# Attention heads in pairs, nine tokens of one head per partition, one burst in row halves, and MLP sums in borrowed PSUM banks

## The chip, the cores and the metric

The kernel runs on one core of a Trainium2 chip. The metric is the device time of one execution, in microseconds (us), as the median over the executions of a kernel.

Engines have short names. PE is the matmul engine (TensorE) and PEld is its weight load. DVE is VectorE, ACT is ScalarE, POOL is GpSimd and SP is SyncE. PSUM is the memory that PE sums into, and it is divided into banks.

## The reference, cut to what matters

```python
def phi(x):                                   # x: q or k times a scale
    proj = np.einsum('bhsd,md->bhsm', x, omega)      # 64 -> 128 features
    h = proj - np.sum(x * x, axis=-1, keepdims=True) / 2.0
    h = h - np.max(h, axis=-1, keepdims=True)
    return np.exp(h) / np.sqrt(m)
q_p, k_p = phi(q_s), phi(k_s)                 # 8 batches, 8 heads, 576 tokens
kv  = np.einsum('bhsm,bhsd->bhmd', k_p, v)    # called k'v below
z   = np.sum(k_p, axis=2)
out = einsum(q_p, kv) / (einsum(q_p, z) + 1e-06)
x   = out as 4608 tokens x 512
g   = h * sigmoid(1.702 * h), with h = x @ w_in  # 512 -> 2048, "first layer"
y   = g @ w_out                                  # 2048 -> 512, "second layer"
```

## The kernel before

The MLP works in nine blocks of 512 tokens. One chunk of its first layer is four 128x512 matmuls into a PSUM bank (`ph`), a tanh on ACT (`th`), and a gate on DVE (`gT`), which reads `th` and `ph`. The attention of later tokens is woven between these matmuls. From block 2 on, PE does the first layer of block i, the second layer of block i-1, and the attention of four pairs of heads (one batch) in the same stretch. I call the part of that stretch that belongs to one pair of heads a round.

Attention runs head by head. k lies with six tokens per partition on 96 partitions. The projections use the two row halves of PE (64 rows each), and k'v uses all rows. The division of k' by its maximum is moved onto v (`vp`).

```python
ps_pp = ctx.enter_context(tc.tile_pool(name="ps_pp", bufs=2, space=PSUM))
ps_m = ctx.enter_context(tc.tile_pool(name="ps_m", bufs=1, space=PSUM))
banks = [ctx.enter_context(tc.tile_pool(name=f"ps_b{j}", bufs=1, space=PSUM)) for j in range(3)]
# (cut) item_qk, one head:
        pk = ps_pp.tile([128, 2, 512], F32, name="pk", tag="pp")
        pq = ps_pp.tile([128, 2, 512], F32, name="pq", tag="pp")
        for c in range(3):
            for lo in (0, 64):
                nc.tensor.matmul(pk[:, lo // 64, c * 128 : (c + 1) * 128], lhsT=kT[lo : lo + 64, ...], rhs=omT2[lo : lo + 64, :])
        for lo in (0, 64):
            nc.tensor.matmul(pq[:, lo // 64, 0:S2], lhsT=omT2[lo : lo + 64, :], rhs=qT[lo : lo + 64, :])
        for _ in range(warmers):     # 6 fillers a head in the head of the program
            nc.tensor.matmul(pq[:, 0, S2:512], lhsT=warm[:, 0:128], rhs=warm[:, S2:512])
        # (cut) exp of k and q on ACT; maximum, reciprocal and v' on DVE or POOL
# (cut) item_kv:
            for t in range(6):
                nc.tensor.matmul(kv[:, i, :], lhsT=ke[:, t, :], rhs=vp[:, t, :], start=(t == 0), stop=(t == 5))
# (cut) the MLP's first layer: one-bank tiles, shared with nobody from block 1 on
            phs[i, f] = banks[j].tile([128, TB], F32, name="ph", tag=f"b{j}")[:]
```

The softmax here doesn't subtract the row's maximum and nothing guards it: scores larger than these inputs give would overflow.

## Time and profile before

| | before |
|---|---|
| median of 2 runs | 338.39 us (337.62 to 339.16) |
| span of the profiled run | 335.6 us |
| PE busy | 96% |
| first tanh of block 0 / block 2 / block 7 | 28.45 / 91.67 / 264.12 us |

The starts of the tanh instructions on ACT are used here to cut the span into stages: a head, an early part up to block 2, and a steady part.

First, lines of the profile's page: the span, busy time by engine, PE and clock by 40 equal slices (in tenths; 9 means 90% or more), and the chain of waits.

```profile
span 335.6 us, 6767 instructions
...
PE 322.2 (96%) x2562; PEld 170.1 (51%) x2606; DVE 229.8 (68%) x551; ACT 203.0 (60%) x363; POOL 83.4 (25%) x162
...
PE   7999899999999999999999999999999999999996
...
PEclk9999999999999999999999999999999999999999
...
PE 78%; DMA 10%; ACT 4%; DVE 4%; issue 2%; POOL 1%; SPq 0%; POOLq 0%; ACTq 0%; DVEq 0%
```

PE is busy at full clock nearly everywhere, and the chain that ended last is 78% PE. A change has to take work off PE.

The list of what PE waited for (waiting instruction, what released it, us in total, times, longest us) shows no wait that repeats in every round. Its two largest entries:

```profile
PE warm_ps L90 <- DVE warm L86: 1.5, 1, 1.5
PE kv L240 <- POOL vp L226: 1.2, 3, 0.5
```

The timeline shows the attention of one pair among the MLP's matmuls (start, duration, engine, line, tiles, count).

```profile
138.42 0.35 PE L185 MATMUL pk<-omT,qk 64*128 64x128 bf16 x6
...
141.69 0.35 PE L185 MATMUL pk<-omT,qk 64*128 64x128 bf16 x6
...
142.97 0.55 PE L240 MATMUL kv<-vp,ke 96*128 96x65 bf16 x12
```

Each head has its own burst of projections (the six for k are shown). One stretch of twelve k'v matmuls follows for the pair.

### The profile page before, as it was taken

The numbers are of one execution on the slowest core, as the hardware profiler recorded it, in microseconds if no ns is written. First come the engines' busy times: TensorE is split into PE (matmuls) and PEld (weight loads), VectorE is DVE, ScalarE is ACT, GpSimd is POOL, SyncE is SP. The second block draws the span as 40 slices with busy tenths as digits, with TensorE's granted clock in tenths as the row PEclk, the third lists the DMA queues.
The fourth block names the chain that finished last, engine by engine and source line by source line (L and its number), as shares of the span: only waits on it lengthen the run. The fifth ranks groups of instructions, "written<-read, shape, count | busy, mean of one in ns | idle before, by whom it ended". The sixth has DMA issues, their size and how long they took to land.

```text
span 335.6 us, 6767 instructions
## 1 busy us (share of the span) xinstructions
PE 322.2 (96%) x2562; PEld 170.1 (51%) x2606; DVE 229.8 (68%) x551; ACT 203.0 (60%) x363; POOL 83.4 (25%) x162
## 2 busy tenths in 40 slices
PE   7999899999999999999999999999999999999996
PEld 3764455554445444555445555554545444444444
DVE  2887886989888877887788868886887334444300
ACT  4977867778766656665666666665665444344411
POOL 8882455302250115111511041000101011001010
PEclk9999999999999999999999999999999999999999
DMA  8999998997699619993898269941212110101022
GB/s 180 238 227 255 249 187 124 163 236 139 91 219 186 139 47 219 192 128 76 198 195 155 66 155 182 193 92 51 51 51 50 51 31 31 64 31 31 33 73 84
DMA packets 59412, 43.31 MB, mean 129 GB/s; under 512 B 44020, under 2 KB 54260, under 8 KB 58740
## 3 DMA queue, kind: packets, MB, share of 16 engines
q0 software_dynamic: 10320, 21.86, 32.3%
q1 hardware_dynamic: 48852, 20.72, 30.8%
q8 instruction: 20, 0.33, 0.4%
q10 hardware_dynamic: 208, 0.29, 0.3%
q14 instruction: 12, 0.10, 0.1%
HBM read 36.73 MB, written 15.34 MB: 155 GB/s over the span
## 4 chain that ended last, share of the span: by engine, by line
PE 78%; DMA 10%; ACT 4%; DVE 4%; issue 2%; POOL 1%; SPq 0%; POOLq 0%; ACTq 0%; DVEq 0%
PE po L351 33%; PE ph L325 30%; DMA qk<-in_q_dram 5%; PE pk L185 4%; PE kv L240 3%; PE nd L255 2%; DMA xt<-xb 2%; PE pq L191 2%; DMA out_dram<-osb 2%; ACT ke L195 1%; DMA qk_f<-in_k_dram 1%; ACT qe L197 1%; PE po L372 1%; PE pq L193 1%; POOL vp L220 1%
## 5 line engine op out<-in xcount | busy, mean ns | idle before, releaser
L325 PE MATMUL ph<-xt,win 128*128 128x512 bf16 x555 | 145.9, 380 | 2.5 <-DVE gT L339 0.5
L351 PE MATMUL po<-wout,gT 128*128 128x512 bf16 x537 | 139.0, 379 | 2.0 <-issue 0.5
L338 ACT ACTIVATE th<-ph 128x512 bf16<-128x512 f32 x144 | 85.7, 598 | 87.7 <-PE ph L325 86.0
L339 DVE SCALAR_TENSOR_TENSOR gT<-th,ph 128x512 bf16<-128x512 bf16 x144 | 97.1, 679 | 58.1 <-ACT th L338 55.7
L325 PEld LDWEIGHTS <-win 128*128 128x128 bf16 x576 | 59.3, 114 | 50.6 <-issue 5.5
L351 PEld LDWEIGHTS <-gT 128*128 128x128 bf16 x560 | 50.1, 98 | 55.9 <-issue 5.8
L363 POOL DMA_DIRECT2D out_dram<-osb x44 | 23.3, 533 | 174.8 <-ACT osb L360 140.6
L195 ACT ACTIVATE ke<-pk 96x768 bf16<-96x768 f32 x64 | 51.4, 803 | 13.9 <-PE pk L185 13.9
L197 ACT ACTIVATE qe<-pq 128x576 bf16<-128x576 f32 x64 | 41.3, 646 | 1.1 <-PE pq L193 1.1
L258 DVE TENSOR_TENSOR xb<-nd,rden 128x320 bf16<-128x320 f32 x64 | 31.1, 486 | 1.3
L360 ACT ACTIVATE osb<-po 128x512 f32<-128x512 f32 x35 | 20.9, 598 | 16.0 <-PE po L351 15.7
L220 POOL TENSOR_TENSOR vp<-vst,emax 96x384 bf16<-96x384 f32 x20 | 16.6, 830 | 36.7 <-PE ph L325 20.5
L214 DVE TENSOR_REDUCE maxE<-half 96x6 f32<-96x384 bf16 x44 | 24.2, 549 | 1.4
L220 DVE TENSOR_TENSOR vp<-vst,emax 96x384 bf16<-96x384 f32 x44 | 24.3, 552 | 1.0
L255 PEld LDWEIGHTS <-qe 128*128 128x128 bf16 x320 | 17.7, 98 | 13.7 <-DVE xb L258 1.7
L213 DVE TENSOR_TENSOR half<-ke 96x384 bf16<-96x384 bf16 x44 | 15.6, 354 | 10.9 <-ACT ke L195 10.8
L240 PEld LDWEIGHTS <-ke 96*128 96x128 bf16 x384 | 16.7, 98 | 8.5 <-issue 2.9
L240 PE MATMUL kv<-vp,ke 96*128 96x65 bf16 x384 | 19.1, 194 | 1.8 <-POOL vp L226 1.2
L255 PE MATMUL nd<-kvs,qe 128*128 128x65 bf16 x320 | 20.3, 194 | 0.6 <-DVE xb L258 0.6
L210 DVE TENSOR_REDUCE maxE<-ke 96x6 f32<-96x768 bf16 x20 | 18.8, 940 | 2.7 <-ACT ke L195 2.7
L185 PEld LDWEIGHTS <-qk 64*128 64x128 bf16 x240 | 7.3, 102 | 16.9 <-issue 16.9
L257 DVE RECIPROCAL rden<-nd 128x5 f32<-128x5 f32 x64 | 11.8, 185 | 3.4 <-PE nd L255 3.1
(48 smaller groups left out, 192.5 us busy)
## 6 DMA issues: line engine op xcount, KB each, us to landing
vst<-in_v_dram SPq DMA_DIRECT2D x5, 1152.0 KB, 7.7
out_dram<-osb POOLq DMA_DIRECT2D x12, 256.0 KB, 2.3
sk<-in_k_dram POOLq DMA_DIRECT2D x20, 144.0 KB, 7.3
sq<-in_q_dram POOLq DMA_DIRECT2D x20, 144.0 KB, 7.7
vst<-in_v_dram SPq DMA_DIRECT2D x4, 576.0 KB, 13.2
win<-in_moe_w_in_dram POOLq DMA_DIRECT2D x2, 1024.0 KB, 14.5
wout<-in_moe_w_out_dram POOLq DMA_DIRECT2D x4, 512.0 KB, 17.8
out_dram<-osb POOLq DMA_DIRECT2D x10, 192.0 KB, 2.7
```

The costliest lines, as they stand in the source:

```text
L195: nc.scalar.activation(out=ke[:], in_=pk[0:KP, :, 0:384], func=AF.Exp, scale=SCALE)
L197: nc.scalar.activation(out=qe[:].rearrange("p (two r) -> p two r", two=2), in_=pq[:, :, 0:S2], func=AF.Exp, scale=SCALE,)
L214: nc.vector.reduce_max(out=maxE[:], in_=half[:], axis=AX.X)
L220: eng.tensor_tensor(out=vp[:, :, 0:64].rearrange("p (two c) d -> p two c d", two=2), in0=tiles[b]["v"][:, h, :].rearrange("p (c two d) -> ...
L240: nc.tensor.matmul(kv[:, i, :], lhsT=ke[:, t, :], rhs=vp[:, t, :], start=(t == 0), stop=(t == 5))
L255: nc.tensor.matmul(nd[:, t, :], lhsT=qe[:, c0 : c0 + 128], rhs=kvs[:, i, :])
L258: nc.vector.tensor_tensor(out=xb[:, :, i * 64 : (i + 1) * 64], in0=nd[:, :, 0:64], in1=rden[:].unsqueeze(2).to_broadcast([128, NCH, 64]), ...
L325: nc.tensor.matmul(ph, lhsT=win[f // 8][:, c, f % 8 // 4 * 512 + f % 4 : (f % 8 // 4 + 1) * 512 : 4], rhs=xt[c][:, i * TB : (i + 1) * TB], ...
L338: nc.scalar.activation(out=th[:], in_=ph, func=AF.Tanh, scale=0.851)
L339: nc.vector.scalar_tensor_tensor(out=gT[:, f, :], in0=th[:], scalar=1.0, in1=ph, op0=ALU.add, op1=ALU.mult)
L351: nc.tensor.matmul(po[:], lhsT=gT[:, f, r * 128 : (r + 1) * 128], rhs=wout[:, f, :], start=(f == 0), stop=(f == NFC - 1),)
L363: eng.dma_start(out[row : row + (n - 1) * step + 1 : step, :], osb[p0 : p0 + n, :])
```

## The change

The intent is less PE time for attention and less work on DVE. Two heads share the 128 partitions, 64 each, with nine tokens per partition. All row-half work of a pair is then one burst: nine k projections, the q projections, and the k'v of the pair before as two streams of nine matmuls in the two halves. Matmuls of different halves may run side by side, and the change into and out of half mode is paid once a pair.

The burst needs wide PSUM tiles, so the banks are cut anew. There are three two-bank tiles (`kp`, `qp`, `xx`) and two single banks. Between bursts, MLP sums borrow the two banks of `kp` as the two halves of one tile (`f:kp`, `f:kp+`). The fillers in the head are dropped.

```diff
+    psum = {
+        n: ctx.enter_context(tc.tile_pool(name=f"ps_{n}", bufs=1, space=PSUM))
+        for n in ("kp", "qp", "xx", "b0", "b1")
+    }
-    WARMERS = 6
...
+    def item_tr(p, home=None, on_act=(False, True)):
+            both = bank("qp", [128, 2, 1024], BF16, "tps")
+            tpk, tpq = both[:, 0, :], both[:, 1, :]
...
+        copy(on_act[0], kT[:], tpk[:, 0:640])
...            six transposes of q into tpq
+        copy(on_act[1], qT[:], tpq[:, 0 : 2 * S2])
...
+    def item_burst(p, kvp=None):
+        for s in range(2):
+            row = [(56, lambda s=s, j=j: proj_k(s, j)) for j in range(4)]
+            row.append((216, lambda s=s: proj_q(s, False)))
+            row.append((29, lambda s=s: proj_q(s, True)))
+            if s == five:
+                row.append((56, lambda s=s: proj_k(s, 4)))
+            if kvp is not None:
+                row += [(30, mm) for mm in kv_mms(xx, kvp, s)]
...            the two rows are issued merged by their times
+        nc.scalar.activation(out=ke[:, 0:8, :]..., in_=pk[:]..., func=AF.Exp, scale=SCALE)
+        nc.scalar.activation(out=qes[:, :, :, 0:256], in_=pq[:]..., func=AF.Exp, scale=SCALE)
+        nc.scalar.activation(out=ke[:, 8, :], in_=xx[:, five, 256:384], func=AF.Exp, scale=SCALE)
...
     def mm1(i, f, c0=0, c1=CM):
+            if homes[i, f][-1] == "+" and (i, f - 1) in readers:
+                for reader in readers[i, f - 1]:
+                    tc.declare_no_dep(mm.ins, reader.ins.name, reason="another PSUM bank")
...
+        readers[i, f] = [
+            nc.scalar.activation(out=th[:], in_=ph, func=AF.Tanh, scale=0.851),
+            nc.vector.scalar_tensor_tensor(
+                out=gT[:, f, :], in0=th[:], scalar=1.0, in1=ph, op0=ALU.add, op1=ALU.mult
+            ),
+        ]
...
+    R5 = "B f:b0 f:b1 T N f:kp X f:b0 f:b1 "
+    ROUND = "B q f:b1 q N f:kp X q f:kp+ q f:b1 "
```

In a round, B is the burst, q is four second-layer matmuls, f is a first-layer chunk with its bank, N is the numerators (the matmuls of q' with k'v), X is the transpose of x, and T is the transposes of the next pair. The framework orders accesses by tile. For the second half of a two-bank tile, PE's matmul does not depend on the readers of the first half.

## The prediction

> **What bounds it now.** TensorE. The profile's first part has PE 96% busy (DVE 68%, ACT 60%), the clock row is at full speed, and the chain of waits is 78% PE. In the timeline a 128x512 matmul follows the last after 216 ns; 1,152 of them make 249 of the 335.6 us. From 92 us on PE hardly waits: blocks of 128 MLP matmuls and four head pairs follow each other every 34.6 us, and their parts add to 34.4. Before 92 us waits are spread (DVE, POOL, loads).
>
> **A pair on PE now** (starts in the timeline): projections 500 ns a head, of which about 190 is the change into row halves and back; k'v 12 matmuls, 32 ns apart, 0.39 us; numerators 10 at 30 ns, 0.31 us. Together 1.70 us. The Trainium skill, "TensorEngine Tiling (Array Packing)", Key Properties, says that a change of tiling mode drains the engine; the trace agrees (95 ns each way).
>
> **After.** One burst per pair: 9 instead of 12 k projections, and k'v in row halves too, 18 matmuls in 9 slots. Row-half partners start 4 ns apart in this trace (pk, pq), as "TensorE: Matmul & The Clock Gate", Part 3, The mechanism, describes; that 65-column ones do too is my assumption. Estimate: 5x56 + 216 + 29 + 9x30 = 0.80 us, plus 0.19 of changes; with numerators 1.30. So 0.40 us less per pair, all critical while PE bounds: 1.6 to 1.75 us per block, about 7 us from 92 us to the end.
>
> DVE gets lighter: per round of one pair (8.2 us of PE), from traced durations scaled by size, about 6.0 us instead of 7.7. The loop "exp of k, max, reciprocal, v', gate, x, gates, then the PSUM banks return" takes about 7.9 us: under 8.2, but the slack is only 0.3 us.
>
> **What it gives back.** One bank pair each for k, q and the mixed sums, shared with MLP sums, so a burst cannot overlap the exp of the previous pair.
> - Head (to the fourth chunk of the first sums): now 27.1 us, estimated 29 to 30. ACT needs 2.3 us a pair in series, the x multiply holds the next burst, and the fillers that kept PE warm are gone.
> - First second-layer phase (six pairs with transposes): transposes wait for the exp of q in the same banks, about 0.5 us a pair.
> - Second block's first layer: 6.1 us of PE per round, but a DVE loop of 7 to 8 us; some 5 us of waits in three rounds.
> Estimate: block 2 starts at about 94 us instead of 92.
>
> **Sum.** -7 in the steady part, +2 before it: 333 us, within 328.5 and 338.5. Faster by over 2%: 0.35; within 2%: 0.61; slower: 0.04.
>
> **What would show each step right or wrong.**
> - k'v matmuls in a burst: partners 4 ns apart, 30 ns per pair (wrong if 60).
> - Blocks 2 to 5: a period of 32.8 us (wrong if above 34).
> - PE idle before pk, tps and ph rises in the list of waits, and lies before 95 us; block 2 starts at 93 to 95 us.
> - DVE busy falls from 230 to about 190 us.
> - Clock row: perhaps under full in the first 20 us.
>
> **What would make it wrong.** Row-half weight loads taking turns: k'v then costs 0.27 us more a pair, and little gain stays. The DVE loop being longer than I add up: every round waits, no gain. Early stages overlapping better than estimated: 328 us. A cold clock or late loads in the head: 337 us.

## More of the kernel before

Nearly all executions were in the fast state. One of the kernel before, in the rounds of e9 and e10, was slow, and the ratios leave it out.

Before, tanh waits for PE alone.

```profile
ACT th L338 <- PE ph L325: 86.0, 106, 1.5
```

## The result, and the profile after

| | before | after |
|---|---|---|
| median of 2 runs | 338.39 us | 349.54 us (349.48 to 349.60) |
| ratio after / before | | 1.0323, 95% interval 1.0261 to 1.0385 |
| span of the profiled run | 335.6 us | 347.6 us |
| DVE busy / ACT busy | 229.8 / 203.0 us | 197.3 / 192.1 us |
| first tanh of block 0 | 28.45 us | 32.08 us |
| first tanh of block 2 | 91.67 us | 106.01 us |
| first tanh of block 7 | 264.12 us | 276.79 us |

Ratios are the mean time of one kernel's fast runs over that of the other's fast runs of the same rounds, so they are not quite the ratio of the medians quoted.

The change is slower by 3%, where the prediction expected 333 us. By the stages, the head cost 3.6 us more and the early part 10.7 us more. The steady part from block 2 to block 7 gained only 1.7 us, and the rest 0.7 us. The sum is, to rounding, the 12.0 us by which the spans differ.

The same lines of the page after:

```profile
span 347.6 us, 6606 instructions
...
PE 312.5 (90%) x2605; PEld 169.9 (49%) x2642; DVE 197.3 (57%) x374; ACT 192.1 (55%) x356; POOL 76.0 (22%) x140
...
PE   7568977777889999999999999999999999999995
...
PEclk9759999999999999999999999999999999999999
...
PE 34%; DVE 33%; ACT 22%; issue 7%; DMA 2%; SPq 0%; ACTq 0%; DVEq 0%
```

PE is busy for 10 us less (6.0 us of that are the 48 dropped fillers, so busy time is not the gain; the period of a round, used below, is the better measure). But the chain that ended last is only 34% PE. It now runs through DVE and ACT. Early in the span, the clock row falls to 7 and 5. The list of PE's waits:

```profile
PE pk L251 <- DVE gT L405: 7.4, 20, 1.1
PE tps L186 <- DVE kT L197: 5.4, 7, 1.3
...
PE tps L180 <- ACT qe L287: 2.2, 4, 0.8
PE ph L386 <- DVE gT L405: 1.7, 4, 0.6
```

The burst (`pk`) waits for a gate 20 times. By the trace, 17 of these lie after 118 us, about 0.3 us each, one in every round of the steady part. ACT, too, waits for something new:

```profile
ACT th L404 <- PE ph L386: 66.1, 66, 1.9
ACT th L404 <- DVE gT L405: 38.4, 24, 1.9
```

Tanh needs only its matmul sum. Yet it waits 24 times for a gate, 38.4 us in total; 18 of these waits, one a round, lie after 118 us. The chain of waits through one whole round shows where (start, duration, what):

```profile
146.03 0.43 PE pk L251 x8
146.48 1.02 ACT ke L281
147.51 0.91 ACT qe L287
...
148.62 0.47 DVE half L311
...
149.11 0.77 DVE maxE L312
...
150.83 0.18 DVE vp L326
151.01 0.57 DVE gT L405
...
151.75 0.82 DVE xb L339
152.57 0.61 DVE gT L405
...
153.26 0.61 ACT th L404
...
153.89 0.70 DVE gT L405
...
154.63 0.21 PE pk L251
```

From burst to burst it is 8.60 us, and PE's own MLP matmuls are not in it. The chain goes through the exps of k and q, the maximum (L311, L312), v', a gate, and x, with short steps left out here. Then it goes to the gate of the first half of `kp` (at 152.57), the tanh of the second half (153.26), the gate of the second half (153.89), and the next burst. The tanh at 153.26 is the surprise. Its sum was done at 152.60 us (151.57 plus 1.03), but it stood behind the gate of the other half, as the timeline says in brackets (idle before, and what ended it):

```profile
151.57 1.03 PE L386 MATMUL ph<-xt,win 128*128 128x512 bf16 x4
...
152.49 0.68 DVE L405 SCALAR_TENSOR_TENSOR gT<-th,ph 128x512 bf16<-128x512 bf16 x1
...
153.26 0.60 ACT L404 ACTIVATE th<-ph 128x512 bf16<-128x512 f32 x1 [1.75 <-DVE gT L405]
```

The PE side did what was hoped:

```profile
146.03 0.42 PE L251 MATMUL pk<-omT,qk 64*128 64x128 bf16 x8 [0.31 <-DVE gT L405]
...
146.53 0.47 PE L203 MATMUL xx<-vp,ke 64*128 64x65 bf16 x18
```

Eighteen k'v matmuls now take less time than twelve did (0.47 us against 0.55 us, each with the end of the last one). By the single records, the starts run from 146.530 to 146.814 us, about 33 ns for each pair of partners.

### The profile page after: what moved, and what is told of

Its sections match the earlier page's. It is cut to its first block, busy times and chain, and to the rows that moved or that the text cites. A ratio compares the mean times of both kernels' runs of the same rounds, so it can differ in the third digit from the quotient of the medians.

```text
span 347.6 us, 6606 instructions
## 1 busy us (share of the span) xinstructions
PE 312.5 (90%) x2605; PEld 169.9 (49%) x2642; DVE 197.3 (57%) x374; ACT 192.1 (55%) x356; POOL 76.0 (22%) x140
## 4 chain that ended last, share of the span: by engine, by line
PE 34%; DVE 33%; ACT 22%; issue 7%; DMA 2%; SPq 0%; ACTq 0%; DVEq 0%
PE po L416 14%; DVE gT L405 14%; PE ph L386 12%; ACT qe L287 8%; ACT ke L281 7%; DVE xb L339 6%; DVE maxE L312 5%; ACT th L404 5%; DVE half L311 4%; PE pk L251 3%; DMA xt<-xb 2%; ACT ke L293 2%; DVE emax L317 1%; PE xx L335 1%; PE warm_ps L88 1%
## 5 line engine op out<-in xcount | busy, mean ns | idle before, releaser
L311 DVE TENSOR_TENSOR half<-ke 128x576 bf16<-128x576 bf16 x32 | 15.1, 471 | 45.1 <-ACT ke L293 45.1
L281 ACT ACTIVATE ke<-pk 128x1024 bf16<-128x1024 f32 x32 | 32.8, 1025 | 8.6 <-PE pk L251 7.2
L287 ACT ACTIVATE qe<-pq 128x1024 bf16<-128x1024 f32 x32 | 32.6, 1020 | 0.0
L339 DVE TENSOR_TENSOR xb<-xx,rden 128x640 bf16<-128x640 f32 x32 | 26.4, 823 | 1.4 <-DMA xt<-xb 0.4
L312 DVE TENSOR_REDUCE maxE<-half 128x9 f32<-128x576 bf16 x32 | 24.1, 753 | 0.9
L320 DVE TENSOR_TENSOR vp<-vst,emax 128x576 bf16<-128x576 f32 x25 | 18.9, 757 | 0.9
L335 PE MATMUL xx<-kvs,qe 128*128 128x65 bf16 x320 | 15.8, 198 | 3.3 <-ACT qe L296 2.9
L203 PE MATMUL xx<-vp,ke 64*128 64x65 bf16 x576 | 16.0, 194 | 1.8 <-DVE xb L339 1.3
L251 PE MATMUL pk<-omT,qk 64*128 64x128 bf16 x160 | 8.4, 219 | 6.7 <-DVE gT L405 6.7
L203 PEld LDWEIGHTS <-ke 64*128 64x128 bf16 x576 | 13.1, 97 | 2.6 <-issue 2.4
```

The lines of the kernel that those rows point to most:

```text
L203: yield lambda t=t: nc.tensor.matmul(xx[:, i, 64:129], lhsT=ke[lo : lo + 64, t, :], rhs=vp[lo : lo + 64, t, :], start=(t == 0), stop=(t == ...
L251: return nc.tensor.matmul(dst, lhsT=kcols(r, j), rhs=omT2[r : r + 64, :])
L281: nc.scalar.activation(out=ke[:, 0:8, :].rearrange("p (c s) f -> p s c f", s=2), in_=pk[:].rearrange("p s (c f) -> p s c f", c=4), func=AF ...
L287: nc.scalar.activation(out=qes[:, :, :, 0:256], in_=pq[:].rearrange("p s (i r) -> p s i r", i=2), func=AF.Exp, scale=SCALE,)
L311: nc.vector.tensor_tensor(out=half[:], in0=ke[:, :, 0:64], in1=ke[:, :, 64:128], op=ALU.max)
L312: nc.vector.reduce_max(out=maxE[:], in_=half[:], axis=AX.X)
```

## The experiments

Theory A is that the steady loss is a false wait. Both halves of a two-bank tile count as one tile, so the tanh of one half waits for the gate of the other, which stands late in DVE's queue. Rival B is that DVE or ACT is really full, or PE needs 8.6 us a round, so that taking the wait away moves nothing. Theory C, in the expectations below, is that the burst itself or its shared banks cost more than thought. For the early part there were several candidates: the same kind of wait among transposes, the clock, and the loads. Results of all runs were correct. "Period" is the time from burst to burst in blocks 2 to 6. The table gathers the experiments (times in us; ratios against before). A stage time is the start of the first tanh of that block in the profiled run.

| run | median | ratio (95%) | period | block 0 | block 2 | block 7 |
|---|---|---|---|---|---|---|
| after | 349.54 | 1.0323 (1.0261 to 1.0385) | 8.61 | 32.08 | 106.01 | 276.79 |
| e1_tanh | 340.93 | 1.0031 (0.9974 to 1.0089) | 8.27 | 32.15 | 103.87 | 268.59 |
| e2_transposes | 348.93 | 1.0286 (1.0212 to 1.0359) | 8.61 | 31.49 | 104.95 | 275.73 |
| e3_both | 339.70 | 1.0000 (0.9934 to 1.0065) | 8.27 | 31.77 | 100.86 | 265.54 |
| e5_ke8 | 349.49 | 1.0279 (1.0221 to 1.0338) | 8.61 | 31.01 | 105.09 | 275.88 |
| e5b_ke8 | 343.81 | 1.0144 (1.0102 to 1.0186) | 8.27 | 31.60 | 106.00 | 270.86 |
| e6_warm | 339.02 | 1.0001 (0.9942 to 1.0060) | 8.27 | 30.31 | 101.64 | 266.36 |
| e7_casts | 338.02 | 0.9991 (0.9933 to 1.0048) | 8.27 | 32.07 | 100.33 | 265.05 |
| e8_all | 339.18 | 0.9982 (0.9918 to 1.0045) | 8.27 | 30.54 | 102.32 | 266.99 |
| e9_loads | 334.56 | 0.9898 (0.9873 to 0.9922) | 8.27 | 30.04 | 97.06 | 261.78 |
| e10_order | 332.91 | 0.9847 (0.9823 to 0.9870) | 8.27 | 30.32 | 95.48 | 260.16 |
| e11_serial | 337.19 | 0.9919 (0.9870 to 0.9968) | 8.45 | 30.41 | 96.28 | 264.20 |
| e12_bank | 330.81 | 0.9732 (0.9690 to 0.9774) | 8.27 | 29.99 | 93.02 | 257.70 |

The runs were made in four sets of rounds on four chips (e1 to e5; e5b to e8; e9 and e10; e11 and e12). The kernel before ran along in each, and its median there was 339.64, 338.98, 338.51 and 340.06 us. So a difference of a microsecond between runs of different sets may be the chip's, and each stage time is that of one execution. From the second round of block 2 on, the periods repeat from round to round within 0.02 us.

### e1_tanh: take the wait between halves away, nothing else

```diff
+        if homes[i, f][-1] == "+" and (i, f - 1) in readers:
+            for reader in readers[i, f - 1]:
+                for one in (tanh, gate):
+                    tc.declare_no_dep(one.ins, reader.ins.name, reason="another PSUM bank")
```

The wait may be removed because the halves lie in different banks. The Trainium skill, "PSUM — Partial Sum Buffer", section "PSUM bank collisions raise a hardware error", says that two engines collide when they touch one bank in the same group of 32 partitions, while accesses to different banks run clean. All executions of this and the later kernels with the edit gave correct results, which agrees.

> One thing changed in the kernel after: the tanh and the gate of the second half of a two-bank sum no longer count the readers of the first half as something to wait for. Theory A (the changed kernel is held by a wait between two PSUM halves: the tanh of the second half waits for the gate of the first, which stands behind v' and x on DVE): the period of blocks 2 to 6 falls from 8.61 to 8.2-8.3 us, the first block's first layer (31.7 to 45.3 us) gets about 2 us shorter; 338 to 342 us, ratio to before 1.00-1.01. Theory B (the DVE loop of a round is simply too long in work): period stays at 8.6, ratio stays about 1.03. Theory C (the row-half burst itself costs more than thought, or bank sharing between the burst and the first-layer sums does it): period stays at 8.6.

The time fell by 8.6 us and the period from 8.61 to 8.27 us. The order of instructions on ACT, DVE and POOL is that of after, so only the wait differs. In the timeline the two gates now run one behind the other, tanh waits for PE, and the burst starts without a wait:

```profile
157.22 1.36 DVE L404 SCALAR_TENSOR_TENSOR gT<-th,ph 128x512 bf16<-128x512 bf16 x2
157.26 0.60 ACT L403 ACTIVATE th<-ph 128x512 bf16<-128x512 f32 x1 [1.13 <-PE ph L386]
...
158.88 0.42 PE L251 MATMUL pk<-omT,qk 64*128 64x128 bf16 x8
```

The chain that ended last is PE's again:

```profile
PE 79%; DVE 7%; ACT 7%; DMA 2%; issue 2%; SPq 1%; ACTq 0%; DVEq 0%
```

Theory A holds, and B and C fall, for the steady part. DVE is busy for 5.78 us of a round both here (of 8.27 us) and in after (of 8.61 us), so DVE was not full; it was waiting.

### e2_transposes: the same for the transposes of q, alone

```diff
-        copy(on_act[0], kT[:], tpk[:, 0:640])
+        k_read = copy(on_act[0], kT[:], tpk[:, 0:640])
...            for each transpose of q, tq:
+                if home is None:
+                    tc.declare_no_dep(tq.ins, k_read.ins.name, reason="another PSUM bank")
...
+        q_read = copy(on_act[1], qT[:], tpq[:, 0 : 2 * S2])
+        if home is None:
+            tc.declare_no_dep(q_read.ins, k_read.ins.name, reason="another PSUM bank")
```

In after, the six transposes of q (L186) wait for the copy of k out of the other bank of their tile:

```profile
59.16 0.44 PE L180 MATMUL tps<-ident,qk 128*128 128x128 bf16 x5 [0.47 <-ACT qe L287]
...
59.69 0.48 DVE L197 COPY kT<-tps 128x640 bf16<-128x640 bf16 x1
...
60.22 0.41 PE L186 MATMUL tps<-ident,qk 96*128 96x96 bf16 x6 [0.63 <-DVE kT L197]
```

> One thing changed in the kernel after: the transposes of q and the copy of q out of PSUM no longer count the copy of k (which reads the other bank of the same tile) as something to wait for. Theory A2 (the same kind of wait costs in the second-layer phase of block 0): PE idle before the q transposes goes from 5.4 us to near 0, the seven rounds from 45 to 82 us shorten by 0.3 to 0.6 us each; 344 to 347 us, ratio 1.017-1.027. Rival (that phase is held by the exp of q and by v', the transposes only fill a gap): less than 1 us gained, ratio 1.03. The period of 8.61 us later is not touched under either.

The list of waits gave 5.4 us to this, but only about 1 us came back by block 2. The three rounds from the first burst of the second-layer phase shrank from 5.57, 5.88 and 5.01 us to 4.78, 5.11 and 4.23 us. Later rounds gave most of it back to other waits, for x (PE's wait for it ahead of the short q projections rose from 1.5 to 4.2 us) and for v' made on POOL. The run does not separate well from after. My expectation was too high, and what came is the rival's: less than 1 us gained. A sum of waits on PE is not the gain from removing them.

### e3_both: both edits

The diff is that of e1 and e2 together.

> The changes of e1 and e2 together. If both waits are real and apart in time, the gains add: about 10 to 14 us less than the kernel after, 335.5 to 339 us, ratio 0.99-1.003. If they share one cause further back, less than the sum.

The two gains add: 9.8 us by the medians, where e1 has 8.6 and e2 0.6 us (a little less than expected). The steady part is cured: block 2 to block 7 takes 164.7 us against 170.8 us after and 172.5 us before. The early part is still 9.2 us behind before. One round there took 8.32 us. In its timeline PE waits 1.26 us for v' on POOL, which is standing behind the issuing of loads, and a row of four 128x512 matmuls takes 1.91 us in place of 1.03 us. That is the clock at half.

```profile
59.66 0.19 PE L206 MATMUL xx<-vp,ke 64*128 64x65 bf16 x1 [1.26 <-POOL vp L329]
...
62.00 1.91 PE L422 MATMUL po<-wout,gT 128*128 128x512 bf16 x4
```

### e5_ke8 and e5b_ke8: shorten the loop elsewhere and keep the false wait

The exp of the ninth token of k stands behind the long exp of q, so the maximum waits for both. If the round is limited by the loop through the false wait, moving that exp ahead by 0.9 us must shorten the round, although the wait stays. This tests theory A without touching what e1 touched.

```diff
+        nc.scalar.activation(out=ke[:, 8, :], in_=xx[:, five, 256:384], func=AF.Exp, scale=SCALE)
         nc.scalar.activation(out=qes[:, :, :, 0:256], ...)
-        nc.scalar.activation(out=ke[:, 8, :], in_=xx[:, five, 256:384], func=AF.Exp, scale=SCALE)
```

> One thing changed in the kernel after: the exp of the ninth token of k (128 columns) is done on ACT ahead of the exp of q (1024 columns) instead of after it. Theory A (a loop through ACT and DVE sets the period): DVE can begin its max 0.9 us earlier in each round, so the period falls to 8.2-8.3 us with the false wait still there, and the rounds from 45 to 82 us shorten by some 0.3 us; 339 to 343 us, ratio 1.002-1.014. Theory B with DVE work alone as the limit, or theory C: period stays at 8.6.

The run of e5 is void as a test. ACT's order is set by the framework's scheduler, and in all but the first two pairs it put the instruction back to where it was, so the period stayed 8.61 us. In e5b the order was held by hand:

```diff
+        with tc.manual_schedule(engines={ET.Activation}):
             ... the four exps, the ninth token's second
```

> What e5 was meant to be, with ACT's order of the five burst readings held to the program's (in e5 the scheduler put the ninth token's exp back behind the exp of q, so that run changed nothing): the false wait between halves stays. Theory A (loop from the freed k banks through exp of k, ninth token, max, v', gate, x, gate of half 1, tanh and gate of half 2, back to the k banks): the loop gets 0.9 us shorter, so the period of blocks 2 to 6 falls from 8.61 to the 8.27 us that e1 showed PE alone to need; about 341-343 us, ratio 1.003-1.013. If the period stays at 8.6, the loop does not run through the max and theory A has a hole.

The period is 8.27 us although the false dependency is still declared. It no longer holds anything up in the steady part: the first half's gate now ends at 167.43 us, before the second half's sum is done, and tanh waits for PE. Of the 24 waits of tanh for a gate, the six that are left lie before 96 us:

```profile
ACT th L405 <- DVE gT L406: 6.0, 6, 1.1
...
167.65 0.60 ACT L405 ACTIVATE th<-ph 128x512 bf16<-128x512 f32 x1 [1.13 <-PE ph L387]
```

Two different cuts of the same loop give the same floor, so the loop was the limit and 8.27 us is what PE itself needs. Block 2 starts at 106.00 us, as after does: the edit cures the steady part and nothing early.

### e6_warm: e3 with fillers in the head

```diff
+    def fill(n):
+        two = bank("kp", [128, 2, 512], F32, "fill")
+        for m in range(n):
+            nc.tensor.matmul(two[:, m % 2, :], lhsT=warm[:, 0:128], rhs=warm[:])
...            25 in all, between the first bursts and transposes
```

> On e3: 25 filler matmuls (216 ns each at full clock) in the head's PE gaps, into the k banks, which stand free there. Theory H1 (the head lost time because its PE gaps let the clock drop to half: the clock row shows 0.7 and 0.5 in slices 2 and 3): the clock row stays at 9 and the first tanh comes at 29.5-30.5 us instead of 31.8, 337.5-338.5 us. Theory H2 (the head is bound by ACT and DVE in series, one bank pair each): the clock row recovers but the first tanh moves by less than 0.5 us.

The same stretch in after and in e6, by windows of 4 us (columns: window, its length, busy time of PE, PEld, DVE, ACT and POOL with counts, then the granted clock as a share of full, DMA share, GB/s):

```profile
10.00:14.00 4.00, 2.02 (x45) 1.57 (x43) 3.58 (x8) 3.97 (x8) 1.77 (x4) 0.99 1.10 279
14.00:18.00 4.00, 2.54 (x31) 2.23 (x31) 2.64 (x6) 0.50 (x4) 2.83 (x5) 0.50 1.16 208
```

```profile
10.00:14.00 4.00, 3.43 (x50) 2.05 (x48) 3.38 (x7) 3.91 (x9) 2.52 (x4) 1.00 1.12 282
14.00:18.00 4.00, 3.38 (x63) 2.24 (x61) 3.01 (x7) 1.00 (x4) 2.59 (x5) 1.00 1.14 207
```

In after the clock is half from 13.9 to 27.5 us. With the fillers it stays full, and the first tanh comes 1.5 us earlier than in e3. The other runs agree: it comes at 31.01 to 32.15 us in the seven kernels without fillers and at 29.99 to 30.54 us in the six with them. The clock in the head was therefore a real but small cost. The time as a whole did not move: in a later round of 8.12 us DVE waited 2.30 us for an earlier transfer of x before it could make the next, PE waited behind it, and the gain was gone.

### e7_casts: e3 with the loads of batch 3 issued later

```diff
-            12: [lambda: load_bc(3)],
+            21: [lambda: load_bc(3)],
```

> On e3: batch 3's eight cast loads are issued on POOL nine steps later, behind the v' of pairs 6 and 7 instead of ahead of them. Theory: in e3 v' of pair 6 starts about 1 us after its reciprocal because POOL stands at DMA issues, PE then idles and drops to half clock, and one round takes 8.3 us instead of 5. Expect that round at 5-5.6 us and the clock row at 9 in slices 7 and 8: 335.5-337.5 us, 2 to 3 us less than e3. Rival (the round is held by x on DVE): still 8 us.

The round of 8.32 us became 5.71 us, so POOL's issuing in front of v' was its cause. But the next long round is 9.63 us, where the first layer waits 1.5 us for the transpose of x by DMA, and the burst 1.4 us for x. The total is unchanged within the interval.

### e8_all: e3, e6 and e7 together

> e3, e6 and e7 together. If they are apart in time, gains add: 333-336 us, ratio to before 0.98-0.995, steady period still 8.27.

There was no gain in the median. (One of the four executions took 335.68 us at a clock of 0.999, within the expectation; the traced one took 339.72 us.) All loads of batch 3 are now issued at once at about 61 us, just before the transposes of x. One of these was issued at 61.94 us and landed at 76.29 us, and a round of 13.1 us followed, in which the clock row shows 6.

```profile
61.94 1.34 SPq L360 DMA_TRANSPOSE xt<-xb  x1
...
76.33 0.59 PE L389 MATMUL ph<-xt,win 128*128 128x512 bf16 x1 [2.20 <-DMA xt<-xb]
```

In this stretch (61 to 79 us), six of these transposes take a median of 8.7 us to land:

```profile
xt<-xb SPq DMA_TRANSPOSE x6, 8.7
```

### e9_loads: e6 with loads spread out

The loads of batch 2 are issued under the first block's first layer. The casts of batch 3 are issued one pair per round, and v of batch 3 follows later.

```diff
+        1: [lambda: load_begin(2), lambda: load_k(2, 0, 1), lambda: load_q(2, 0, 1), lambda: load_v(2, 0, 2)],
+        3: ...  5: ...  7: ...            (pairs 1 to 3)
...
-            12: [lambda: load_bc(3)],
+            1: [lambda: load_begin(3), lambda: cast_k(3, 0, 1), lambda: cast_q(3, 0, 1)],
+            8: ...  15: ...  21: ...      (one pair each)
...
+        3: [lambda: load_v(3, 0, NPAIR)]
```

> On e6 (both false waits gone, fillers in the head): batch 2's loads go one stage earlier, under the first block's first layer; batch 3's cast loads are spread one pair per round behind v' on POOL, and its v load comes after the x transposes of batch 1. Theory: in e8 the gain of the faster rounds was lost because eight casts and v (3.5 MB) were issued together at 61 us and the x transposes that block 1 needs took 14 us to land instead of 2.4. Expect no round before block 2 over 8.2 us, clock row at 9 throughout, first tanh of block 2 at 96-98 us (e3: 100.9, e8: 102.3), 332-335 us, ratio 0.98-0.99. Rival (the early part is bound by the chain ACT, DVE, POOL of a pair in one bank set): it stays at 100 us and over.

Six transposes from 55 to 72 us here take a median of 4.3 us. Not all of them are the six above, but the four that both kernels issue between 61.8 and 69.4 us took 8.0 to 14.3 us in e8 and 2.3 to 4.8 us here. The clock is full throughout, and block 2 starts 4.6 us earlier than in e6. Three groups of loads were moved at once, so this run does not tell which of them mattered.

```profile
xt<-xb SPq DMA_TRANSPOSE x6, 4.3
```

### e10_order: e9 with e5b's order on ACT

The diff is e5b's.

> e9 with the ninth token's exp ahead of the exp of q on ACT (as e5b). The steady period is PE-bound at 8.27 in e9, so it stays; the DVE-bound rounds of block 1's first layer (7.8 and 8.0 us in e3) may lose up to 0.9 us each, the transposes of the second-layer rounds (which wait for the exp of q) may lose 0.2 us each: within 2 us of e9 either way.

Block 2 starts at 95.48 us, 1.6 us earlier. The two long rounds of the second block's first layer are 7.04 and 7.43 us, where e9 has 7.83 and 8.04 us. The steady period does not move, as it is PE's.

### e11_serial: e10 with the two k'v streams one after the other

This measures the disputed part of the PE side: whether 65-column matmuls of two row halves really run side by side.

```diff
-                order.append((at, s, mm))
+                order.append((at + 300 * (s == 1 and ns == 30), s, mm))
```

> e10 with the k'v matmuls of the two row halves issued one half after the other instead of in turn; nothing else. Theory (the gain of the burst is that partners in the two row halves run at once): a burst lasts 9 x 30 ns = 0.27 us longer, so the period goes from 8.27 to 8.5-8.55 us and the time up by 6 to 8 us to 339-341 us, no better than before. If halves do not really run at once in k'v: the period stays at 8.27.

The period rose by 0.18 us over e10's, and the span of the profiled run from 331.0 to 335.0 us. That is less than expected, because the two streams still overlap for a few matmuls in the middle. The starts now run over 0.440 us, one about every 33 ns in the stretches of one half alone, against 0.321 us in e10. From the start of the burst to the last k'v start it is 1.00 us, against 0.82 us in e10; the difference is the 0.18 us. Side-by-side k'v is therefore worth at least 0.18 us a pair.

### e12_bank: e10 with transposes in other banks

In the second-layer phase of the first block, the transposes wait for the exp of q in their banks (`qp`). The exp of k in `kp` is done sooner.

```diff
-                    item_tr(p)
+                    item_tr(p, both="kp" if i is None else "qp")
```

> e10 with the transposes of the second-layer rounds put into the k banks (free after the exp of k and the ninth token's) instead of the q banks (free 0.9 us later). PE's wait for the exp of q before tps (3.6 us in 6 places in e10) goes to near 0; if nothing else takes its place, 330-331.5 us; if the rounds are held by x on DVE or v' on POOL as well, less than 1 us gained.

The median is 330.81 us in six runs, and the ratio to before is 0.9732: faster than both kernels. (The kernel before took longer in the rounds of this run, 340.06 us; against its 338.39 us in the first rounds the ratio of medians is 0.978.) PE's wait for the exp of q ahead of `tps`, 3.6 us in e10, is gone from the list. The span and the clock on its page:

```profile
span 328.6 us, 6684 instructions
...
PEclk9999999999999999999999999999999999999999
```

## Why the prediction was wrong, point by point

**The step that failed: "The loop … takes about 7.9 us: under 8.2, but the slack is only 0.3 us."** The loop that I added up left out a step, the tanh of the second half between the two gates. In after the first gate of `kp` starts at 152.49 us and the second at 153.89 us, 1.40 us apart. In e1 two such gates take 1.36 us together, so 0.68 us apart. The false wait is thus 0.72 us a round, and 8.60 less 0.72 is 7.88 us: the loop that I predicted, without the wait. The trace of e1 agrees: the second gate ends 7.97 us after the burst's start, 0.30 us before the next burst, so the slack of 0.3 us was there once the wait was gone. With it the loop passes PE's 8.27 us, and each round waits. I had read in the diff that PE's matmul was freed from the readers of the other half, and did not ask whether tanh and gate were. The text did name this among what would make it wrong: "The DVE loop being longer than I add up: every round waits, no gain." That is what came. e1 removes the wait and e5b shortens the loop elsewhere, and both give 8.27 us.

**The blocks.** "Blocks 2 to 5: a period of 32.8 us (wrong if above 34)" gave 34.4 us (four rounds of 8.61). With e1 it is 33.1 us. The estimate of PE's own part, 8.2 us a round, was right within 0.1 us.

**The second step that failed: "block 2 starts at about 94 us instead of 92."** Measured: 106.01 us, so 14.3 us late where I had 2.3. This is the larger part of the miss: 12 us, where the steady part missed by 5.3 us (-1.7 for -7). The losses that I listed (two to three us in the head, six times 0.5 us, some 5 us) add to more than the 2 us that I netted them to, and the text names no gain to set against them. Measured by the first tanhs of blocks 0, 1 and 2, the losses are 3.6 us in the head, 5.3 us in block 0 and 5.4 us in block 1; they simply add. The experiments split the cause as follows, by the start of block 2; each line is one kernel against another, and the amounts depend on the order of the edits:

- False waits between halves (e3 against after): 5.2 us. They act in the first block's first layer, where tanh and gate alternate, and in the transposes.
- Fillers and the spreading of loads (e9 against e3): 3.8 us. Fillers alone, and later casts alone, gave nearly nothing in the total, since each gain met the next wait. Loads pushed together (e8) lost it.
- Order of the exps (e10 against e9): 1.6 us, and other banks for transposes (e12 against e10): 2.5 us.

What is left in e12 is 1.4 us over before. I had listed the wait for the exp of q, the chain through DVE and late loads. The false waits were not on the list. Taken together, early and steady, they are worth 11.2 us of span (e3 against after), nearly all of the 12.0 us lost.

**The head.** To the fourth chunk of the first sums I estimated 29 to 30 us instead of 27.1. It was 31.7 us; to the first tanh it was 3.6 us more (28.45 to 32.08 us). Of this, 1.5 us is the clock by e6 against e3. I wrote "perhaps under full" and it was half from 13.9 to 27.5 us.

**The PE side was right.** That partners in two row halves start 4 ns apart I took from "TensorE: Matmul & The Clock Gate", Part 3, "The mechanism"; the 30 ns a slot came from traced matmuls. The traces agree: in the steady bursts of e1, e10 and e12 the k'v partners start 0 to 7 ns apart, with 33 ns from one pair to the next. In after, where the burst was released by a gate, one half ran 40 to 42 ns behind the other in 17 bursts (by the q projections), at the same 33 ns a pair. The period of a pair fell from 8.64 us in before (34.57 us a block) to 8.27 us in e1: 0.37 us, where I wrote 0.40. e11 shows that the overlap matters. The warning of row halves "taking turns" did not come true.

**DVE** fell to 197.3 us ("about 190"), and to 5.78 us a round ("about 6.0").

**PE's waits** rose at `pk`, `tps` and `ph` as written, but not only "before 95 us": 17 of the 20 waits of `pk` for a gate lie in the steady part.

**The sum.** "-7 in the steady part, +2 before it" was wrong for the kernel as written, and is near what its mended form e12 reaches. e12 against before has -7.8 us from block 2 to block 7, +1.4 us before it, and -0.6 us after it. The span is 7.0 us shorter. For after the same terms are -1.7, +14.3 and -0.7. But e12 also has other loads, banks and an order on ACT that were not tried on before, so it is not a test of the idea alone.

Two things stay open. The split of the early part among its causes is only as good as the order in which they were undone, and rests on single executions (e3's traced one was the fastest of its four, by 1.2 us). And why the clock in the head fell just then is only argued: the fillers prevent it, but no run varies the length of the gaps.

## What to carry to other kernels

When a tile spans several PSUM banks, look at every engine that touches a part of it: a freed matmul is not enough if tanh, gate or copy of one part still waits for a reader of another, and such a dependency costs nothing while that reader is done in time (e5b), but holds up every round when the reader stands late in a loop. When you add up a loop to compare it with PE's period, include the waits that the framework makes, not only those of the data: with 0.3 us of slack in 8, a wait of 0.72 us was enough to turn the limit around. In a stage with many small waits, the sum of a wait in the profile is not its worth: remove the causes together and move loads away from short transfers on which PE waits.

## What the Trainium skill lacked or had wrong

- "TensorE: Matmul & The Clock Gate", Part 1 and "Why this matters for your kernels", ties the drop to half clock to an idle window of about 3.4 us, and advises against gaps above about 3 us. In after the clock was half from 13.9 to 27.5 us with no gap of PE above 1.5 us. From 10 to 14 us PE was busy for 2.02 of 4 us, 0.71 us of it transposes, with gaps of at most 1.13 us. With fillers (3.43 of 4 us busy, no gap above 0.8 us in the head) the clock stayed full. The page's section on depth-cycling does speak of small idles but gives no size. No run here separates the length of the gaps, the busy share and the kind of matmul.
- The same page, Part 3, "The mechanism", gives partners of different row groups starting 4 ns apart, and the runs agree (0 to 7 ns for 65-column partners in e1, e10 and e12). I found nothing there on a burst that has been waiting: in after, whose bursts waited for a gate, one half ran 40 to 42 ns behind, where e1's and e10's, which did not wait, show 0 to 4 ns (q projections). Why is not shown.
- No page that I found says that waits are made per tile, so that parts of a tile in different banks hold each other up; "PSUM — Partial Sum Buffer" gives only the rule of bank and partitions that makes the wait needless. Here it cost 0.72 us in the loop of each round (0.34 us of the period), and 8.6 us of 349.5 in all for tanh and gate (e1).
- "DMA: Bandwidth & Descriptors", "Queues, rings and completion order", says that a DMA engine takes its queues in turn, but gives no size for what a short transpose loses among large loads. Here the same four transposes took 8.0 to 14.3 us to land among them (e8) and 2.3 to 4.8 us when the loads were spread (e9).
